# A hand-written order of attention and feed-forward work is rewritten behind its first 204 operations; weights' sums go in halves to two engines, two norms are ended on VectorE

## The chip, the cores and the metric

The kernel runs on one core of one Trainium2 chip. Its engines are PE (TensorE, matrix products; its weight loads are listed as PEld), DVE (VectorE), ACT (ScalarE), POOL (GpSimd) and SP (SyncE, which here only issues DMAs). Each engine takes its own instructions strictly in the order in which the program issued them, and waits at one whose data are not there. The metric is the device time of one execution in microseconds.

## The reference, cut to what matters

```python
# q, k, v: (8, 12, 448, 64); w_in: (768, 2048); w_out: (2048, 768)
q_n = q / (np.linalg.norm(q, axis=-1, keepdims=True) + 1e-06)
k_n = k / (np.linalg.norm(k, axis=-1, keepdims=True) + 1e-06)
scores = np.matmul(q_n, k_n.transpose(0, 1, 3, 2)) / tau          # tau = 0.1
scores = scores - np.max(scores, axis=-1, keepdims=True)
attn = np.exp(scores)
attn = attn / (np.sum(attn, axis=-1, keepdims=True) + 1e-09)
x = np.matmul(attn, v)             # its 12 heads side by side: (3584, 768)
h = x @ w_in
g = h * np.clip(h + 3.0, 0.0, 6.0) / 6.0
out = g @ w_out
```

## The kernel before, in words

**Attention.** The 8 x 12 heads are worked as 48 pairs, numbered 0 to 47, six to a batch. Queries and keys of two neighbouring pairs are loaded together as one "twin" item j, in even and odd j (`load_qk`, LQ). Values are loaded for two pairs (`load_v`, LV). For an item, the squares are taken (`square`, SQ, on the engine that the plan names: a = ACT, p = POOL, v = DVE), summed on DVE (`reduce`, RE), and turned into reciprocal norms for two items at once by four ACT activations, logarithms and exponentials (`norms`, NO, L252 to L255). The raw item is multiplied by them (`normalise`, NM), and transposed: up to item 13 by PE (`transposes`, TR, then copies out of PSUM, CQ for queries, CK and CS for keys), from item 14 on by a DMA (`crossbar`, XD, issued by SP, then CK on DVE and CS on POOL, L372). `vcast` (VC) makes the bf16 values.

For pair i there are four groups of scores, SC.i.0 to SC.i.3. Each of the first three is two matmuls of 64 rows each that run side by side; the fourth is one of 128 rows. `exps` (EX, ACT) follows each, two instructions for each of the first three groups and one for the fourth; `values` (VA, PE) multiplies by the values into the one bank PV, eight matmuls a group; `finish_values` (FI, DVE) divides and makes the bf16 output `on`. That is transposed into xT, the input of the first product, by PE and a copy (BK, CX) or by DMA (XB for one pair, XP for two).

**Feed-forward.** `unit` (U) is PE's next piece of the two products with w_in and w_out. In the plan there are 36: U1 to U30 are six matmuls of 448 columns each (L566), followed by one ACT instruction (UA, L575) and one DVE instruction (UV, L581). U31 to U36 are sixteen matmuls of 384 columns each (L613), copied out in turn by ACT (UA, L624) and by DVE (UV, L626) and stored by two DMAs from SP. UA and UV take the oldest unfinished unit. Later, in the loop, the second product is worked with sums of blocks of g and of w_out (`g_sum`, L717, and `weight_sums`, WS, L688), seven products in place of eight. `weight_sums` makes three arrays, 6, 1 and 7, and overwrites two blocks of w_out in place, y3 and y4; y3 overwrites columns that U31 to U33 read, y4 columns that U34 to U36 read. The second half of y4 is made in the loop (L861).

**PSUM.** Behind OPEN (L925), every score group (two banks, or one for the fourth), unit, TR and BK takes the next of six banks in turn: M0, M1, Y, Z, M2, M3, and again. PE can write one only when the last reader of what stood there is through.

**What sets the order.** `PLAN` (L21) is a list of 611 operations written out by hand, run one after another by `run` (L959). The program's order on each engine follows from it alone. It ends in the turn of pair 17. A loop over the pairs 18 to 47 follows, whose order is fixed in code, with the units of each pair from `TURNS` (L853) and the sums from `side`. DP.n is n dummy matmuls into an unused part of PV (L921). W issues the next part of the weights on POOL's queue. GL copies left-over columns of g.

Of the kernel before, what the change touches and what calls it, by code (L numbers as in the profile page):

```python
# [10 lines left out]
AF = mybir.ActivationFunctionType  # L11
# [3 lines left out]
EPS = 1e-6  # L15
# [46 lines left out]
def kernel(  # L62
# [10 lines left out]
    nc = tc.nc  # L73
    B, H, S, D = q.shape
# [29 lines left out]
    KC = FCN // 2  # L104
# [34 lines left out]
    def raw_buffer(j):  # L139
# [104 lines left out]
    def norms(d, *items):  # L244

        needs(("NM", 2 * d - 4), ("NM", 2 * d - 3))
        items = items or (0, 1)
        for x in items:
            needs(("RE", 2 * d + x))
        it = slice(items[0], items[-1] + 1)  # L250
        ln, nr, le, r = (t[:, it, :] for t in rs[d % 2])
        nc.scalar.activation(out=ln, in_=n2s[d % 2][:, it, :], func=AF.Ln)  # L252
        nc.scalar.activation(out=nr, in_=ln, func=AF.Exp, scale=0.5)
        nc.scalar.activation(out=le, in_=nr, func=AF.Ln, bias=EPS)
        nc.scalar.activation(out=r, in_=le, func=AF.Exp, scale=-1.0)  # L255
        for x in items:
            issued.add(("NO", d, x))

# [411 lines left out]
            return wide[n % 2], wide[2]  # L670
        return wide_late[2 * (n - LOOP) : 2 * (n - LOOP) + 2]

    def weight_sums(what, c0, n):

        w = w_out_sb[:, :, :].rearrange("p (c k) m -> p c k m", k=2)[:, c0 : c0 + n]
        b11, b12, b21, b22 = (w[:, :, k, m] for k in range(2) for m in (LEFT, RIGHT))
        for x in {"y3": "16", "y4": "17"}.get(what, ""):
            assert all((x, c) in summed for c in range(c0, c0 + n))
        o, x, y, op = {
            "1": (b11, b11, b22, ALU.add),  # L680
            "6": (b11, b11, b12, ALU.add),
            "7": (b21, b21, b22, ALU.add),
            "y3": (b12, b12, b22, ALU.subtract),
            "y4": (b21, b21, b11, ALU.subtract),
        }[what]
        if what in w_sum:
            o = w_sum[what][:, c0 : c0 + n, :]
        nc.vector.tensor_tensor(out=o, in0=x, in1=y, op=op)  # L688
# [250 lines left out]
    def whole_units(n, engines="av"):  # L939
# [153 lines left out]
```

## Time and profile before

| what | value |
|---|---|
| median of the runs shown | 405.85 us (405.72 to 407.1, 3 runs) |
| the profiled execution's own time | 405.02 us |
| its span, first to last instruction | 403.24 us |
| granted TensorE clock over the span | 1.00 |
| SC.6.0, the first matmul of the plan's ring of six banks, starts | 34.96 us |
| SC.18.0, the loop's first score matmul, starts | 114.64 us |
| last PE unit of the plan (U36) starts | 111.70 us |
| ACT, square of one item | 0.95 us, x8 |
| POOL, square, and product, of one item | 1.69 and 1.72 us, x36 and x44 |
| DVE, product of one item | 1.09 us, x2 |
| DVE, sums of weights (L688), wholes and halves | 0.95 to 3.24 us, x7 |

Durations are of one execution. A mean in the table of groups covers all instructions of one line and shape. In a timeline, each line gives start, length, engine, line, operation, what is written and read, the shape and the number of instructions merged; in brackets stands idle time before it and who ended it. An instruction's length is from its start to its end, so two that follow at once can overlap a little in it: an exponential is listed with 0.565 us, and the next starts 0.42 after it. In a list of waits stand the engine that waited, what it wanted to write, the engine that came last, and microseconds, times and the longest.

### The profile page before, as it was taken

How to read it: one execution, taken by the hardware profiler on the slowest of the kernel's cores; microseconds unless marked ns; L12 is line 12 of the kernel's file. 1: busy time of each engine (PE TensorE's matmuls, PEld its weight loads, DVE VectorE, ACT ScalarE, POOL GpSimd, SP SyncE). 2: the span in 40 equal slices, each digit the busy share in tenths (PEclk: the TensorE clock that was granted, in tenths of full speed). 3: DMA queues.
4: the chain of work that ended last, by engine and by line, in shares of the span. 5: the costliest groups of instructions: out<-in, count | busy, mean ns of one | idle time of the engine just before them, and what ended most of it. 6: DMA issues, size and time to landing. Idle time of an engine off the chain costs nothing.

```text
span 403.2 us, 9617 instructions
## 1 busy us (share of the span) xinstructions
PE 394.5 (98%) x3696; PEld 233.7 (58%) x3696; DVE 286.4 (71%) x501; ACT 266.2 (66%) x609; POOL 233.2 (58%) x228
## 2 busy tenths in 40 slices
PE   7999999999989999999999999999999999999996
PEld 5666556555655556555555556555565556555564
DVE  6898768766998676776857878687656666644663
ACT  6899998787557686776758768668648755224230
POOL 7899664562294996489386875776665500510070
PEclk9999999999999999999999999999999999999999
DMA  8999989989989559885989659986864523130133
GB/s 290 308 241 276 200 249 239 144 126 221 193 204 231 120 119 228 176 224 130 181 214 210 134 143 171 183 193 145 191 150 82 112 46 67 40 79 20 27 73 99
DMA packets 91566, 65.32 MB, mean 162 GB/s; under 512 B 56064, under 2 KB 89984, under 8 KB 91520
## 3 DMA queue, kind: packets, MB, share of 16 engines
q1 hardware_dynamic: 87408, 58.02, 62.8%
q0 software_dynamic: 3712, 6.29, 9.1%
q8 instruction: 29, 0.48, 0.5%
q10 hardware_dynamic: 400, 0.39, 0.3%
q14 instruction: 17, 0.14, 0.1%
HBM read 47.19 MB, written 11.01 MB: 144 GB/s over the span
## 4 chain that ended last, share of the span: by engine, by line
PE 94%; DVE 3%; DMA 1%; POOL 1%; ACT 0%; issue 0%; SPq 0%; DVEq 0%
PE M L566 24%; PE M L739 17%; PE PV L455 13%; PE Y L566 6%; PE M L415 6%; PE Z L566 5%; PE Y L739 4%; PE Z L739 4%; PE M L613 3%; PE M L819 2%; PE Z L415 2%; PE PV L921 2%; PE Z L819 1%; PE Y L415 1%; PE SC L415 1%; DMA big<-in_q_dram 1%
## 5 line engine op out<-in xcount | busy, mean ns | idle before, releaser
L433 ACT ACTIVATE at<-M 128x448 bf16<-128x448 f32 x200 | 99.6, 565 | 17.7 <-PE M L415 15.5
L566 PE MATMUL M<-xT,w_in_sb 128*128 128x448 bf16 x522 | 110.7, 353 | 0.0
L566 PEld LDWEIGHTS <-w_in_sb 128*128 128x128 bf16 x768 | 71.9, 98 | 62.5 <-issue 2.6
L267 POOL TENSOR_TENSOR nrm<-big,r 128x896 bf16<-128x896 f32 (+1 forms) x48 | 79.4, 1658 | 26.7 <-ACT r L255 18.5
L581 DVE SCALAR_TENSOR_TENSOR gT<-u,M 128x448 bf16<-128x448 bf16 x76 | 46.8, 618 | 35.6 <-ACT u L575 35.3
L455 PEld LDWEIGHTS <-at 128*128 128x128 bf16 (+1 forms) x1536 | 54.8, 97 | 24.1 <-issue 14.8
L224 POOL TENSOR_TENSOR big<-big 128x896 f32<-128x896 f32 (+3 forms) x39 | 63.8, 1639 | 8.0 <-DMA big<-in_k_dram 4.1
L575 ACT ACTIVATE u<-M 128x448 bf16<-128x448 f32 x87 | 48.8, 561 | 29.5 <-PE M L566 29.1
L455 PE MATMUL PV<-vx,at 128*128 128x65 bf16 (+1 forms) x1536 | 64.3, 194 | 0.2 <-DVE on L476 0.2
L236 DVE TENSOR_REDUCE n<-big 128x14 f32<-128x896 f32 (+1 forms) x50 | 51.8, 1040 | 3.9 <-ACT big L222 3.4
L372 POOL COPY km<-tT 64x128 bf16<-64x128 bf16 x34 | 12.4, 364 | 59.3 <-DMA tT<-nrm 43.4
L768 POOL TENSOR_TENSOR big<-big 128x384 f32<-128x384 f32 x11 | 12.0, 1088 | 55.1 <-ACT big L787 55.0
L739 PEld LDWEIGHTS <-gT 128*128 128x128 bf16 x288 | 27.8, 98 | 20.2 <-DVE gT L717 0.6
L739 PE MATMUL M<-w_out_sb,gT 128*128 128x384 bf16 x208 | 37.9, 326 | 0.1
L433 ACT ACTIVATE at<-Z 128x448 bf16<-128x448 f32 x49 | 27.6, 564 | 10.4 <-PE M L415 8.8
L286 POOL CAST vx<-big 128x512 bf16<-128x512 f32 x44 | 33.0, 754 | 2.4 <-DMA big<-in_v_dram 2.4
L476 DVE TENSOR_TENSOR on<-PV,rc 128x512 bf16<-128x512 f32 x48 | 33.2, 691 | 1.7
L415 PE MATMUL M<-tT,kz 64*128 64x448 bf16 (+1 forms) x175 | 31.9, 351 | 1.0 <-DVE o L626 1.0
L739 PEld LDWEIGHTS <-gs 128*128 128x128 bf16 x224 | 21.6, 98 | 14.5
L566 PE MATMUL Y<-xT,w_in_sb 128*128 128x448 bf16 x132 | 28.6, 353 | 0.0
L433 ACT ACTIVATE at<-Y 128x448 bf16<-128x448 f32 x45 | 25.6, 568 | 3.3 <-PE Z L415 3.1
L739 PE MATMUL M<-w_sum,gs 128*128 128x384 bf16 x144 | 26.3, 326 | 0.0
(131 smaller groups left out, 553.9 us busy)
## 6 DMA issues: line engine op xcount, KB each, us to landing
big<-in_v_dram SPq DMA_DIRECT2D x96, 128.0 KB, 4.7
big<-in_k_dram SPq DMA_DIRECT2D x24, 448.0 KB, 4.9
big<-in_q_dram SPq DMA_DIRECT2D x24, 448.0 KB, 4.3
out_dram<-o SPq DMA_DIRECT2D x107, 96.0 KB, 2.2
w_in_sb<-in_moe_w_in_dram POOLq DMA_DIRECT2D x4, 768.0 KB, 9.1
w_out_sb<-in_moe_w_out_dram POOLq DMA_DIRECT2D x4, 768.0 KB, 9.7
tT<-nrm SPq DMA_TRANSPOSE x34, 3.4
xT<-on SPq DMA_TRANSPOSE x25, 3.8
```

Of the source, the lines that this page charges most:

```text
L224: engines[e].tensor_tensor(out=o, in0=i, in1=i, op=ALU.mult)
L236: nc.vector.tensor_reduce(out=n2s[d % 2][:, j % 2, c], in_=sq[:, :, :, :].rearrange("p g c d -> p (g c) d")[:, c, :], axis=AX.X, op=ALU.add,)
L267: engines[e].tensor_tensor(out=nrm[:, :, g, :].rearrange("p c g d -> p g c d"), in0=raw_of[j][:, g, :, :], in1=rs[d % 2][3][:, j % 2, :] . ...
L286: (engines[e].copy if e == "a" else engines[e].tensor_copy)(out=o, in_=f)
L415: nc.tensor.matmul(o, ks, qt[rows], start=True, stop=True)
L433: nc.scalar.activation(out=o, in_=x, func=AF.Exp, scale=inv_tau)
L455: nc.tensor.matmul(pv_out(j, h), at[rows, n, q_cols(i // HP, j)], vt[rows, 3 + h if name == "M" else 5 * h + int(name[1]), :], start=(name ...
L476: nc.vector.tensor_tensor(out=on[:, :, :, :].rearrange("p j h d -> p h j d"), in0=pv4[:, :, :, 0:D], in1=rc[:, :, :].to_broadcast([128, 2, ...
L566: nc.tensor.matmul(ps[:, 0:S], w_in_sb[:, cc, fc * 128 : (fc + 1) * 128], x[:, cc, 0:S], start=(cc == 0), stop=(cc == CC - 1),)
L575: nc.scalar.activation(out=u[:, :], in_=ps[:, 0:S], func=AF.Relu, bias=0.5, scale=1.0 / 6.0)
L581: nc.vector.scalar_tensor_tensor(out=g[:, fc, c0 : c0 + S], in0=u[:, :], scalar=1.0, in1=ps[:, 0:S], op0=ALU.min, op1=ALU.mult,)
L739: nc.tensor.matmul(m, lhs[:, c, :], rhs[:, c, c0 : c0 + width], start=(base is None and c == 0), stop=(c == KC - 1), skip_group_check=True,)
```

## The change

The plan's first 204 operations, up to OPEN, stay. The 407 behind them become 411 in another order. Two dummy operations (DP.2, DP.1, three matmuls) are left out. Several copies, casts and squares go to another engine: CX.3, CX.10, CK.9, CK.13, CS.11, CS.12 from DVE to ACT; CQ.11, CK.12 from ACT to DVE; VC.8, 7, 11, 14, 16 from POOL to DVE and VC.13, 15, 17, 18, 19 from POOL to ACT; SQ.13, SQ.15 from ACT to POOL; SQ.14 from POOL to ACT and, a seventh of it, DVE; SQ.16 wholly to POOL; SQ.19, SQ.21 from POOL to ACT and SQ.22 from DVE to ACT; NM.12 from POOL to DVE, NM.11 in two halves. The norms of the twins 6 and 8 take two steps on ACT (NA) and two on DVE (ND). The sums 1, 6 and y3 are made in halves, as 7 and y4 were, and the first halves of 6 and 7 are made on POOL. The loop is not changed.

```diff
-    "BK.3.Y VA.4.1 LQ.12 CS.6.v OPEN DP.2 CX.3.v NO.5 SC.6.0 VA.4.2 VA.4.3 SC.6.1 SC.6.2 EX.6.0 NM.8.p FI.4 EX.6.1",
-    "EX.6.2 SC.6.3 TR.8 BK.4 VA.5.0 CX.4.v VA.5.1 CQ.8.v SC.7.0 VA.5.2 EX.6.3 NM.9.p CQ.9.v VC.6.p VA.5.3 SC.7.1",
-    "FI.5 EX.7.0 SC.7.2 TR.9 SC.7.3 NM.10.p CK.8.v VA.6.0 EX.7.1 EX.7.2 VC.8.p CS.8.v W BK.5 SQ.12.p.0.7 LQ.13",
-    "VA.6.1 VA.6.2 SC.8.0 EX.7.3 CS.9.v VA.6.3 CK.9.v DP.1 EX.8.0 CX.5.v SC.8.1 SC.8.2 VC.7.p FI.6 LQ.15 EX.8.1 U",
-    "UA SQ.13.a.0.7 LV.5 U TR.10 EX.8.2 UA U RE.13 U SC.8.3 UV UA CQ.10.v VA.7.0 W RE.12 UV CQ.11.a UV UA NO.6 U",
-    "EX.8.3 VA.7.1 VA.7.2 UV VC.9.p VA.7.3 NM.11.p SC.9.0 FI.7 NM.12.p UA SC.9.1 UV EX.9.0 U VA.8.0 SC.9.2 EX.9.1",
-    "VC.10.p UA SC.9.3 TR.11 UV NM.13.p CS.11.v XP.6 VA.8.1 LQ.14 EX.9.2 SQ.15.a.0.7 VA.8.2 U EX.9.3 CK.11.v",
-    "CK.10.v VA.8.3 SC.10.0 TR.12 U CS.10.v FI.8 UA UV VA.9.0 SC.10.1 LQ.17 EX.10.0 SQ.14.p.0.7 CQ.12.v CQ.13.v",
-    "SC.10.2 UA VA.9.1 LQ.19 VA.9.2 EX.10.1 LQ.16 VA.9.3 LV.6 W UV SC.10.3 EX.10.2 U SC.11.0 FI.9 EX.10.3 SC.11.1",
-    "U UA EX.11.0 LV.7 EX.11.1 UV UA SC.11.2 RE.15 BK.8 LQ.18 CX.8.v U VA.10.0 U VA.10.1 UA EX.11.2 UV UV RE.14",
-    "SC.11.3 UA BK.9 VA.10.2 VA.10.3 FI.10 EX.11.3 TR.13 NO.7 CK.13.v CS.13.v CX.9.a U UV CK.12.a VC.11.p W",
-    "VA.11.0 U SC.12.0 CS.12.v VA.11.1 VA.11.2 UA BK.10 VA.11.3 UV UA NM.15.p UV EX.12.0 CX.10.v SC.12.1 EX.12.1",
-    "SC.12.2 FI.11 U EX.12.2 BK.11 SC.12.3 UA NM.14.p SQ.16.p.0.6 U UA CX.11.v UV U SC.13.0 SQ.17.p.0.7 XD.14 UV",
-    "RE.17 EX.12.3 VC.12.p EX.13.0 SQ.16.a.6.1 U UA RE.16 VC.15.p U VA.12.0 UV XD.15 UA U UA UA UV SC.13.1",
-    "SQ.19.p.0.7 VC.13.p SC.13.2 UV EX.13.1 LQ.21 U VA.12.1 VA.12.2 UA UV RE.19 VA.12.3 EX.13.2 UV NO.8 W U",
-    "SC.13.3 NM.16.p CK.15.v CK.14.v U UA UA SQ.18.a.0.7 EX.13.3 U SC.14.0 FI.12 UA VA.13.0 VC.14.p CS.14.v UV",
-    "VA.13.1 UV EX.14.0 UV U SC.14.1 SC.14.2 VA.13.2 VA.13.3 UA EX.14.1 UV U W SC.14.3 FI.13 U VA.14.0 NM.17.p UA",
-    "EX.14.2 UA VA.14.1 EX.14.3 XD.17 U UV VA.14.2 RE.18 SC.15.0 SC.15.1 UA UV EX.15.0 U XD.16 EX.15.1 UA UV",
-    "VA.14.3 SC.15.2 U UA SC.15.3 EX.15.2 FI.14 NO.9 LV.8 VA.15.0 LV.9 UV CK.16.v UV EX.15.3 U SQ.21.p.0.7 VA.15.1",
-    "RE.21 CS.16.v LQ.20 SC.16.0 LQ.22 SC.16.1 UA VC.16.p SC.16.2 VC.17.p VA.15.2 EX.16.0 VA.15.3 XP.12 NM.18.v",
-    "CK.17.v XD.18 U EX.16.1 SQ.20.a.0.7 NM.19.p FI.15 WS.6 U UV XD.19 SC.16.3 RE.20 GL.0 WS.1 WS.7.0 EX.16.2 U VA.16.0 UA VA.16.1 LV.11",
-    "EX.16.3 SC.17.0 UV VC.19.p SC.17.1 SC.17.2 SQ.22.v.0.7 VA.16.2 LQ.23 EX.17.0 VA.16.3 EX.17.1 LV.10 U SC.17.3",
-    "XP.14 NO.10 FI.16 NM.20.p CK.18.v U CK.19.v WS.7.1 WS.y3 WS.y4.0 XB.16 EX.17.2 UV UA VA.17.0 VC.18.p EX.17.3 RE.22 CS.18.v",
+    "BK.3.Y VA.4.1 LQ.12 CS.6.v OPEN NO.5 CX.3.a SC.6.0 VA.4.2 EX.6.0 VA.4.3 FI.4 SC.6.1 EX.6.1 NM.8.p SC.6.2",
+    "EX.6.2 TR.8 SC.6.3 BK.4 VA.5.0 NM.9.p VA.5.1 VA.5.2 EX.6.3 SC.7.0 CQ.9.v VA.5.3 CQ.8.v EX.7.0 CX.4.v SC.7.1",
+    "EX.7.1 SC.7.2 TR.9 FI.5 CK.8.v SC.7.3 VC.6.p VA.6.0 CK.9.a VA.6.1 NM.11.p.1 EX.7.2 W EX.7.3 BK.5 CS.8.v",
+    "CX.5.v VA.6.2 CS.9.v VA.6.3 VC.8.v U UA UV SC.8.0 W EX.8.0 SC.8.1 U VC.7.v EX.8.1 UA NM.10.p U U SC.8.2 FI.6",
+    "UA VA.7.0 LQ.13 TR.10 UA EX.8.2 UV NM.11.p.0 SQ.12.p.0.7 UV SC.8.3 UV CQ.11.v VA.7.1 VA.7.2 CQ.10.v SC.9.0",
+    "SC.9.1 RE.12 LQ.14 SQ.13.p.0.7 EX.8.3 SC.9.2 VA.7.3 EX.9.0 U EX.9.1 FI.7 LV.5 SC.9.3 TR.11 U UA VC.11.v",
+    "CK.10.v CK.11.v CS.10.v VA.8.0 EX.9.2 UV VA.8.1 VA.8.2 EX.9.3 UA XP.6 UV SC.10.0 CS.11.a VC.9.p VA.8.3 RE.13",
+    "SC.10.1 SC.10.2 EX.10.0 EX.10.1 NA.6 U U VC.10.p UA EX.10.2 FI.8 SQ.14.v.6.1 VA.9.0 ND.6 NM.12.v SC.10.3 UA",
+    "VA.9.1 VA.9.2 NM.13.p EX.10.3 LQ.16 UV TR.12 U UV CQ.13.v VA.9.3 SC.11.0 CQ.12.v LQ.15 UA SC.11.1 U FI.9",
+    "EX.11.0 VA.10.0 VA.10.1 VA.10.2 EX.11.1 UV UA SC.11.2 EX.11.2 SQ.15.p.0.7 LV.6 VA.10.3 U SQ.14.a.0.6 LQ.17",
+    "UA UV VC.13.a BK.8 U FI.10 LQ.18 SC.11.3 UA U BK.10 LQ.19 CX.8.v EX.11.3 VA.11.0 VC.12.p UA UV RE.14 TR.13",
+    "RE.15 UV W BK.9 CX.10.a VA.11.1 CK.13.a VA.11.2 CK.12.v VA.11.3 U LV.7 CX.9.a CS.12.a UV CS.13.v FI.11 UA",
+    "SC.12.0 SC.12.1 U UV EX.12.0 BK.11 UA SQ.17.p.0.7 CX.11.v W NO.7 SQ.16.p.0.7 U UV EX.12.1 U RE.16 UA VA.12.0",
+    "SC.12.2 UA SQ.18.a.0.7 UV U NM.15.p EX.12.2 UA U RE.17 UV SC.12.3 VA.12.1 UV VA.12.2 NA.8 UA EX.12.3 UV",
+    "NM.14.p U SC.13.0 UA SQ.19.a.0.7 SC.13.1 XD.14 U UV EX.13.0 U GL.0 VC.15.a UA VA.12.3 ND.8 EX.13.1 UV UA",
+    "FI.12 U UV SC.13.2 NM.16.p UA UV U CK.14.v RE.18 UA U EX.13.2 SC.13.3 UV XD.15 VA.13.0 VA.13.1 CK.15.v W U",
+    "EX.13.3 UA UA SC.14.0 U CS.14.v EX.14.0 UV LQ.22 UA UV LQ.20 W VA.13.2 SQ.20.a.0.7 VC.14.v VA.13.3 SC.14.1",
+    "XD.16 NM.17.p UV SC.14.2 FI.13 U EX.14.1 U VA.14.0 SC.14.3 VA.14.1 EX.14.2 XD.17 UA UA RE.20 EX.14.3 SC.15.0",
+    "U VA.14.2 LV.8 EX.15.0 VA.14.3 WS.1.v.0 UA UV UV SC.15.1 FI.14 LQ.21 SC.15.2 U EX.15.1 WS.6.p.0 LV.9 UV",
+    "WS.6.v.1 SC.15.3 U RE.19 CK.16.v VA.15.0 VA.15.1 UV XP.12 WS.1.v.1 EX.15.2 UA WS.7.v.1 NO.9 SC.16.0 SC.16.1",
+    "CK.17.v EX.15.3 SC.16.2 EX.16.0 VA.15.2 SQ.21.a.0.7 NM.18.v WS.7.p.0 VA.15.3 CS.16.v FI.15 EX.16.1 EX.16.2",
+    "XD.18 U VC.19.a SC.16.3 U NM.19.p VC.16.v XD.19 UA EX.16.3 VA.16.0 WS.y3.v.0 LV.10 VA.16.1 RE.21 SC.17.0",
+    "VC.18.a LQ.23 SC.17.1 UV EX.17.0 EX.17.1 NO.10 SC.17.2 EX.17.2 VA.16.2 VC.17.a VA.16.3 CK.18.v U XP.14",
+    "WS.y3.v.1 SC.17.3 U FI.16 SQ.22.a.0.7 UA WS.y4.v.0 XB.16 UV NM.20.p RE.22 CK.19.v EX.17.3 VA.17.0 CS.18.v",
+    "LV.11",
...
+    def powers(d, *items):
+
+        needs(("NM", 2 * d - 4), ("NM", 2 * d - 3))
+        items = items or (0, 1)
+        for x in items:
+            needs(("RE", 2 * d + x))
+        it = slice(items[0], items[-1] + 1)
+        ln, nr = (t[:, it, :] for t in rs[d % 2][:2])
+        nc.scalar.activation(out=ln, in_=n2s[d % 2][:, it, :], func=AF.Ln)
+        nc.scalar.activation(out=nr, in_=ln, func=AF.Exp, scale=0.5)
...
+    def reciprocals(d, *items):
...
+        nr, le, r = (t[:, it, :] for t in rs[d % 2][1:])
+        nc.vector.tensor_scalar_add(out=le, in0=nr, scalar1=EPS)
+        nc.vector.reciprocal(out=r, in_=le)
...
-    def weight_sums(what, c0, n):
+    def weight_sums(what, c0, n, e="v"):
...
-        nc.vector.tensor_tensor(out=o, in0=x, in1=y, op=op)
+        engines[e].tensor_tensor(out=o, in0=x, in1=y, op=op)
```

In `WS.6.p.0` the letter names the engine and the last number the half (four of eight pairs of row blocks, 1536 columns); `NM.11.p.1` is the second half of an item.

More of the change, by code (lines that the diff above doesn't have):

```diff
@@ L255, in norms @@
         nc.scalar.activation(out=r, in_=le, func=AF.Exp, scale=-1.0)
+        for x in items:
+            issued.add(("NO", d, x))
+    def powers(d, *items):
+        needs(("NM", 2 * d - 4), ("NM", 2 * d - 3))
+        items = items or (0, 1)
+        for x in items:
+            needs(("RE", 2 * d + x))
[3 more added lines that the diff above has]
+        nc.scalar.activation(out=nr, in_=ln, func=AF.Exp, scale=0.5)
+        for x in items:
+            issued.add(("NA", d, x))
+    def reciprocals(d, *items):
+        items = items or (0, 1)
+        for x in items:
+            needs(("NA", d, x))
+        it = slice(items[0], items[-1] + 1)
+        nr, le, r = (t[:, it, :] for t in rs[d % 2][1:])
+        nc.vector.tensor_scalar_add(out=le, in0=nr, scalar1=EPS)
+        nc.vector.reciprocal(out=r, in_=le)
         for x in items:
@@ L946 @@
     OPS = {
-        "LQ": load_qk, "LV": load_v, "W": next_weights, "SQ": square, "RE": reduce, "NO": norms,
+        "LQ": load_qk, "LV": load_v, "W": next_weights, "SQ": square, "RE": reduce, "NO": norms, "NA": powers, "ND": reciprocals,
         "NM": normalise, "VC": vcast, "TR": transposes, "XD": crossbar, "XB": back_crossbar, "XP": back_two, "CQ": copy_q, "CK": copy_k, "CS": copy_k3, "SC": scores,
         "EX": exps, "VA": values, "FI": finish_values, "BK": back, "CX": copy_x, "U": unit, "UA": lambda: finish_units("a"), "UV": lambda: finish_units("v"),
-        "GL": g_left, "WS": lambda x, *h: weight_sums(str(x), *((h[0] * KC // 2, KC // 2) if h else (0, KC))), "UU": whole_units, "D": busy, "DP": busy_pv, "OPEN": open_ring,
+        "GL": g_left, "WS": lambda x, e, *h: weight_sums(str(x), *((h[0] * KC // 2, KC // 2) if h else (0, KC)), e), "UU": whole_units, "D": busy, "DP": busy_pv, "OPEN": open_ring,
     }
@@ L955, in do @@
         key = (op,) + tuple(a for a in args if isinstance(a, int))
-        if op not in ("RE", "NM", "LQ"):
+        if op not in ("RE", "NM", "LQ", "NA", "ND"):
             issued.add(key[:3] if op == "SC" else key)
```

## The prediction

> **What bounds the kernel now.** I read the page's busy line first, then the stages, then who waited for whom on PE, then the timeline around the longest wait.
>
> ```profile
> PE 394.5 (98%) x3696; PEld 233.7 (58%) x3696; DVE 286.4 (71%) x501; ACT 266.2 (66%) x609; POOL 233.2 (58%) x228
> ```
>
> PE is busy nearly always. "Busy" alone could hide waits, as matmuls overlap, so I took the recorded starts of neighbouring matmuls. In a unit of six 448-column products they lie 0.189 us apart, in one of 384 columns 0.1625, in the value products 0.029, again and again with no spread to speak of. So between 34.66 us, where the changed orders part, and the end PE runs without gaps except where a wait is listed. The list for PE from 34 to 122 us has one line:
>
> ```profile
> PE M L415 <- DVE o L626: 1.0, 1, 1.0
> ```
>
> Its place:
>
> ```profile
> 111.34 4.52 DVE L688 TENSOR_TENSOR w_out_sb<-w_out_sb 128x3072 bf16<-128x3072 bf16 x2
> 111.70 2.76 PE L613 MATMUL M<-w_out_sb,gT 128*128 128x384 bf16 x16
> ...
> 115.03 0.35 PE L415 MATMUL M<-tT,kz 64*128 64x448 bf16 x1
> ...
> 115.79 0.54 DVE L626 COPY o<-M 128x384 f32<-128x384 f32 x1
> ...
> 116.39 0.35 PE L415 MATMUL M<-tT,kz 64*128 64x448 bf16 x1 [1.01 <-DVE o L626]
> ```
>
> PE's 36th unit (U36) ends near 114.47. Its bank is copied out by DVE (L626) only behind y3 whole and y4's first half, 4.52 us of sums, and the last score matmul of SC.18.2 needs that bank: it starts at 116.39 instead of 115.03 + 0.19, **1.17 us late**. That is all that can be won by waiting less, up to the later waits of 0.17 (near 120.84) and 0.30 us (near 225). Before 56 us another engine is nearly as full:
>
> ```profile
> 30.00:40.00 10.00, 9.96 (x162) 6.76 (x161) 8.14 (x24) 9.75 (x21) 9.99 (x11) 1.00 1.10 276
> ...
> 100.00:110.00 10.00, 10.00 (x90) 6.20 (x89) 9.60 (x12) 4.84 (x11) 3.33 (x2) 1.00 1.00 208
> ```
>
> After the length come PE, PEld, DVE, ACT, POOL: ACT 9.75 of 10 us there; DVE 9.60 at 100 us, with POOL idle.
>
> **PE's own work.** Both orders hold the same scores, values, transposes and units. The new one leaves out DP.2 and DP.1, three dummy matmuls at 0.106 us: -0.32. Score pairs that stand alone cost a change of shape on both sides: values to scores starts 0.34 us apart against 0.245 for values to values, and scores to values 0.285 against 0.19, 0.19 us per run of scores. Counted in the two orders there are 22 runs before, 21 after: -0.19. Together **-0.50 us**. The floor is no lower than that.
>
> **The first waits.** Without DP.2, SC.6.0 starts at 34.75 (VA.4.1 at 34.41 plus 0.34), and SC.6.1 is due at 34.75 + 0.29 + 2 x 0.245 + 0.10 = 35.63. It writes bank Y, which CX.3 reads. CX.3 was DVE's (35.20 to 35.59) and goes to ACT behind NO.5, whose last instruction starts at 35.12: from about 35.3 with 0.51 us (the one ACT cast to xT) it ends at 35.81, and SC.6.1 starts near 35.86, 0.23 late. Then TR.8, due 35.86 + 0.20 + 0.29 = 36.35, needs NM.8, the second of
>
> ```profile
> 33.12 3.33 POOL L267 TENSOR_TENSOR nrm<-big,r 128x896 bf16<-128x896 f32 x2
> ```
>
> which ends at 36.45 whatever the order: 0.13 to 0.17 late. BK.4 needs the bank that EX.6.1 frees, pushed back by 0.43 on ACT: 0.05. Sum **+0.41 us**: the dummies covered these waits, and leaving them out wins nothing. CK.9 on ACT adds 0.38 before EX.7.2; NO.6 (four steps of 0.26) comes later as two, SQ.13 (0.84) goes to POOL. Following the exponentials at 0.425 each, banks come back 0.0 to 0.3 us ahead of PE until U1, and U5 waits about 0.07. U1 itself comes 0.3 us before CX.5 is done, but only its sixth matmul, 0.95 us on, reads that part of xT: nothing. With ACT this full, a pace 2% off over 10 us adds 0.2, so I keep +0.2 to +0.9 for this part, and take +0.48.
>
> **Norms ended on VectorE.** NA takes two ACT steps (0.52 in place of 1.04); ND is an addition and a reciprocal of 28 columns on DVE, not seen here; nearest is the reciprocal of 8 columns (206 ns), upper end the 614 ns of a 448-column reduce. I take 0.2 each, 0.44 with gaps, twice. NM.12 follows at once on DVE (1.0) and ends about 0.1 us before TR.12 needs it; at the upper end (0.8 more) TR.12 would wait 0.7. [...] NA.8 and ND.8 have 3 us of slack before NM.16.
>
> **Copies moved among DVE, ACT, POOL.** VC on DVE is 0.68 (L284), on ACT about 0.5 (from the 0.94 for 896 columns), each beside PE work of over a microsecond before its values are due. SQ.21 and SQ.22 on ACT stand where ACT was 4.84 to 6.18 of 10 busy. SP issues the same DMAs; XD.14 holds SP until NM.14 (near 75.4), and LQ.22 and LQ.20 behind it land (4.5 us median) some 5 us before SQ.20 asks. LV.11 moves to the end of the plan, its four issues (2.6 us) ahead of XB.17, which has 1.5 us to spare. I cost all this at nothing; if one cover fails it is 0.2 to 0.5 us.
>
> **The sums in halves.** WS on DVE took 1.7 to 2.65 us whole, 0.95 for a half. The difference is POOL:
>
> ```profile
> 99.56 1.68 POOL L267 TENSOR_TENSOR nrm<-big,r 128x896 bf16<-128x896 f32 x1
> 99.60 0.69 DVE L476 TENSOR_TENSOR on<-PV,rc 128x512 bf16<-128x512 f32 x1
> 100.21 2.65 DVE L688 TENSOR_TENSOR w_sum<-w_out_sb 128x3072 bf16<-128x3072 bf16 x1
> 101.19 2.14 POOL L286 CAST vx<-big 128x512 bf16<-128x512 f32 x1
> ```
>
> The sum ends 1.62 us after POOL's product ends (101.24), and POOL's cast (0.61 elsewhere) ends 0.47 after the sum (102.86). The two engines take turns; DVE's product with an input in PSUM (99.60) is not held. [...]
>
> So a POOL half of 1536 columns costs DVE whatever it overlaps. POOL has no such row. From below: products of 448 and 896 columns take 0.94 and 1.68, 0.2 + 1.65 ns a column, 2.7 us. From above: four times the 1.0 of 384 columns with two separate inputs (L768), 4.0. I take 3.4 (0.2 + 4 x 0.8), the row with separate inputs being nearest in kind. [...]
>
> When? Both p halves wait for nothing but POOL's queue: from ND.8 (79.8), NM.16, W, CS.14, W, NM.17 are 1.63 + 0.75 + 0.6 + 0.75 + 1.63 = 5.4, so they run from 85.2 to 85.2 + 2 x 3.4 = 92.0. DVE reaches WS.1.v.0 behind FI.13 and RE.20 at about 91.0, is held 1.0, and the two UV behind it free the bank of SC.15.1 that much later; they had 0.83 to spare. **+0.2 us** (0 at 2.7, +1.4 at 4.0). CS.16 behind them is wanted 9 us later.
>
> **The end.** y3 now lies before U36 in halves (y3.0 at 105, y3.1 at 108). What holds the bank of U36 is y4.0. It overwrites w_out's first chunks, and its compiled wait is on U36's eighth matmul, not its last. In the old trace this can't be seen, as y3 ended at 114.50. The eighth ends 1.5 us after U36's start, y4.0 takes 0.87 alone, so it is over before U36 ends (+2.77); then the copy, 0.54, and 0.06: the bank is free 3.40 after U36's start, PE wants it at 3.33. Left of 1.17: 0.1. **-1.07 us.**
>
> **Sum.** -0.50 + 0.48 + 0.20 - 1.07 = -0.89. The profiled execution (405.02, span 403.24) would come to 404.1; the median of the runs shown lies 0.83 above it, so 405.0 on that scale.
>
> **Rivals.**
> 1. No new wait appears: -0.50 - 1.17, and with the later 0.17 -1.84: 404.0. Against it: NM.8's end at 36.45 is fixed. 0.12.
> 2. The change doesn't do what it says: y4.0 waits for all of U36. Then 0.87 + 0.54 follow 114.47's counterpart, the stall is 0.9 to 1.0 us, and the sum near 0: 405.9. For it: y4.0's start at 114.50 fits U36's end too. 0.12.
> 3. Slower: POOL's halves hold DVE. Place: WS.1.v.0 before the two UV; price 2p - 6.6 us for a half of p us. From p = 3.9 it eats the gain; at 4.5 (L768's longest is 1.5 for 384, so not excluded) it is 2.4 and the time 407.1; over 408 from p = 5.0. For it: the turns in the rows above. Against: 0.94 for 448. 0.14.
> 4. My sum holds: 0.62.
>
> About 0.5% (2.03 us) is what a measurement can tell here. Faster by more, under 403.8, needs rival 1 and a later wait too: 0.06. Slower by more, over 407.9: part of rival 3 and several failed covers at once: 0.11. Within: 0.83. Range 403.8 to 407.5, from rival 1 to rival 3, with the bounds of the first waits and of p.
>
> **What would show it.** Right: PE's list from 34 to 122 us with no wait over 0.3; SC.6.1 behind ACT's cast; TR.8 at about 36.5; SC.18.2's last matmul near 115.1; POOL's L688 at 2.7 to 4.0. Wrong: y4.0 starting at U36's end; DVE's L688 near 91 over 2.5 us with PE waiting at SC.15.1; ACT idle on DVE or DMA at NA, SQ.20 or VC.

## The result, and the profile after

The changed kernel takes **408.15 us** (median of 20 executions, 406.1 to 411.37), the kernel before 405.66 (20, 405.19 to 407.46): ratio **1.0054**, 95% interval 1.0038 to 1.0070, slower. The forecast was 405.0, within 403.8 to 407.5. The profiled execution of after took 408.19 us, span 406.2, mean granted clock 0.994.

The profile page's busy line says little here: PE is busy 1.3 us longer with three matmuls fewer.

```profile
PE 395.8 (97%) x3693; PEld 234.4 (58%) x3693; DVE 286.4 (71%) x506; ACT 269.7 (66%) x617; POOL 229.4 (56%) x219
```

PE's list of waits, from 30 to 142 us, has one line again, but another one. (In the changed file the lines of these operations stand 27 lower: U is L593, scores L442, sums of weights L715; in experiments that lose a line of the plan, 26.)

```profile
PE M L593 <- DMA xT<-on: 2.4, 1, 2.4
```

The old wait is gone, by the mechanism that the forecast gave. The timeline around U36 (start, length, engine, line, operation):

```profile
111.78 2.76 PE L640 MATMUL M<-w_out_sb,gT 128*128 128x384 bf16 x16
...
113.35 0.96 DVE L715 TENSOR_TENSOR w_out_sb<-w_out_sb 128x1536 bf16<-128x1536 bf16 x1 [2.87 <-POOL km L399]
...
114.63 0.56 DVE L653 COPY o<-M 128x384 f32<-128x384 f32 x1 [0.33 <-PE M L640]
...
115.11 0.48 PE L442 MATMUL M<-tT,kz 64*128 64x448 bf16 x2
```

y4.0 starts 1.2 us before U36 ends, just behind U36's eighth matmul (the bracket names a copy on POOL that ended just then; in e12 y4.0 starts 0.1 us behind the eighth matmul again, and 0.3 before that copy ends). The copy follows U36 and not the sum, and SC.18.2's last two matmuls are merged into one line: nothing stands between them. The second of them starts at 115.25; before it was 116.39.

The new wait is 10 us later, at the first unit that reads the part of xT which XB.17 transposes. The timeline of PE there:

```profile
124.70 1.11 PE L593 MATMUL M<-xT,w_in_sb 128*128 128x448 bf16 x5
128.23 0.50 PE L593 MATMUL M<-xT,w_in_sb 128*128 128x448 bf16 x1 [2.42 <-DMA xT<-on]
128.53 2.44 PE L593 MATMUL Y<-xT,w_in_sb 128*128 128x448 bf16 x6
```

Five matmuls run, the sixth waits: its start is 2.77 us behind the fifth's, where 0.189 is usual. And then six matmuls take 2.44 us. In the kernel before the same six took 1.30:

```profile
126.91 1.30 PE L566 MATMUL Y<-xT,w_in_sb 128*128 128x448 bf16 x6
```

The stages of the changed kernel show why (length, busy time of PE, PEld, DVE, ACT, POOL, granted clock, then the DMA engines' share and GB/s; the clock is 1.00 ahead of these):

```profile
125.00:130.00 5.00, 2.58 (x10) 0.98 (x8) 1.42 (x4) 2.13 (x8) 0.71 (x3) 0.83 1.08 223
130.00:135.00 5.00, 5.00 (x45) 2.62 (x44) 2.72 (x5) 2.23 (x6) 5.00 (x5) 0.83 0.95 280
135.00:140.00 5.00, 5.00 (x42) 2.85 (x39) 3.55 (x6) 3.57 (x9) 4.76 (x5) 1.00 0.57 131
```

Behind the wait, eight matmuls start 0.373 us apart instead of 0.189, and one on either side of them 0.29: TensorE ran at half its clock for 3.41 us (granted clock 0.50 from 128.30 to 131.71), and ten intervals took 3.57 us instead of 1.89, **1.68 us** more.

**How the kernels are compared below.** PE's first wait, for the first loads near 10 us, was 0.1 to 2.3 us in the profiles of this study, in code that no kernel here changes. So beside medians I give the *stretch*: from one and the same matmul ahead of the changed orders (33.42 us before, 33.60 after) to the last matmul. Before 365.63, after 368.38: **+2.75**. At the unit above the changed kernel was 1.25 ahead of the one before (124.70 and 125.77, less 0.18 of a later start). Then come +2.58 of waiting and +1.68 of half clock, together +3.01; the remaining -0.26 is won behind it, where the old wait near 225 us (0.30) does not come back. A stretch has scatter of its own: two profiles of one kernel (e3 and e12) differ by 0.65, and kernels that are the same up to 110 us (e1, e2, e6, e7, e13) lose up to there 0 to 1.1 us more than the changed kernel's profile. So a smaller difference than that is read from the waits named beside it. One execution each of e10, e13 and e14 was in a slower state (411.4, 413.1 and 409.97 us): it counts in the medians, not in the ratios.

**Why XB.17 is late** shows in SP's issues. First of before (98.35 is its first output store, the last line XB.17), then of after:

```profile
98.35 1.20 SPq L601 DMA_DIRECT2D out_dram<-o  x2
...
121.45 1.21 SPq L507 DMA_TRANSPOSE xT<-on  x1
```

```profile
96.12 1.72 SPq L209 DMA_DIRECT2D big<-in_v_dram  x2
100.93 1.18 SPq L628 DMA_DIRECT2D out_dram<-o  x2
...
120.89 2.66 SPq L209 DMA_DIRECT2D big<-in_v_dram  x4
123.59 0.59 SPq L197 DMA_DIRECT2D big<-in_k_dram  x1
124.29 1.22 SPq L534 DMA_TRANSPOSE xT<-on  x1
```

XB.17's landing takes the same time (4.0 us before, 3.9 after); the issue is 2.84 us later. From its first store on SP is nearly always issuing, 23.1 us to XB.17 before and 23.4 after, the same transfers in both. But the run starts 2.6 us later. Up to 97.85 SP issues loads; then it stands until 100.93, because in the new order U32's store (its copy on DVE ends at 100.9) is ahead of U31's (copied by ACT at 98.0):

```profile
97.49 0.48 ACT L651 COPY o<-Z 128x384 f32<-128x384 f32 x1 [1.05 <-PE Z L640]
...
100.35 0.56 DVE L653 COPY o<-M 128x384 f32<-128x384 f32 x1 [2.46 <-PE M L640]
```

Theories. **T1**: LV.11's own new place, with its four issues (2.66 us) among the last things ahead of XB.17, makes it late. **T2**: SP is full from its first store on; what counts is when that run starts and how much lies in it, and LV.11 was in it before too. **C1**: the half clock follows from PE's standing still. **C2**: it has another reason.

### The profile page after: what moved, and what is told of

Same layout as the page of the kernel before. It is cut to its first block, busy times and chain, and to the rows that moved or that the text cites. A ratio compares the mean times of both kernels' runs of the same rounds, so it can differ in the third digit from the quotient of the medians.

```text
span 406.2 us, 9628 instructions
## 1 busy us (share of the span) xinstructions
PE 395.8 (97%) x3693; PEld 234.4 (58%) x3693; DVE 286.4 (71%) x506; ACT 269.7 (66%) x617; POOL 229.4 (56%) x219
## 4 chain that ended last, share of the span: by engine, by line
PE 91%; DVE 3%; DMA 2%; ACT 2%; POOL 0%; issue 0%; SPq 0%; ACTq 0%
PE M L593 24%; PE M L766 16%; PE PV L482 12%; PE Y L593 6%; PE M L442 5%; PE Z L593 5%; PE Y L766 4%; PE Z L766 3%; PE M L846 2%; PE M L640 2%; PE Z L442 1%; ACT at L460 1%; PE Z L640 1%; PE Y L442 1%; DMA big<-in_k_dram 1%; PE PV L948 1%
## 5 line engine op out<-in xcount | busy, mean ns | idle before, releaser
L593 PE MATMUL M<-xT,w_in_sb 128*128 128x448 bf16 x522 | 110.6, 353 | 2.4 <-DMA xT<-on 2.4
L593 PEld LDWEIGHTS <-w_in_sb 128*128 128x128 bf16 x768 | 72.4, 98 | 66.9 <-issue 7.7
L226 POOL TENSOR_TENSOR big<-big 128x896 f32<-128x896 f32 (+2 forms) x38 | 62.4, 1645 | 11.5 <-DMA big<-in_q_dram 5.4
L442 PE MATMUL M<-tT,kz 64*128 64x448 bf16 (+1 forms) x171 | 31.5, 351 | 0.0
L593 PE MATMUL Y<-xT,w_in_sb 128*128 128x448 bf16 x138 | 31.0, 362 | 0.0
L460 ACT ACTIVATE at<-Y 128x448 bf16<-128x448 f32 x47 | 26.6, 565 | 3.4 <-PE Z L442 3.3
L313 POOL CAST vx<-big 128x512 bf16<-128x512 f32 x34 | 24.1, 712 | 1.9 <-DMA big<-in_v_dram 1.4
```

The lines of the kernel that those rows point to most:

```text
L226: engines[e].tensor_tensor(out=o, in0=i, in1=i, op=ALU.mult)
L313: (engines[e].copy if e == "a" else engines[e].tensor_copy)(out=o, in_=f)
L442: nc.tensor.matmul(o, ks, qt[rows], start=True, stop=True)
L460: nc.scalar.activation(out=o, in_=x, func=AF.Exp, scale=inv_tau)
L593: nc.tensor.matmul(ps[:, 0:S], w_in_sb[:, cc, fc * 128 : (fc + 1) * 128], x[:, cc, 0:S], start=(cc == 0), stop=(cc == CC - 1),)
```

## The experiments

Stretches are of one profile each; "half clock" counts executions whose mean granted clock was 0.996 or lower, wherever in the execution it fell (in the profiles of e4, e5 and e10 behind the first loads). XB.17's issue is given less the lag of that profile's PE behind the changed kernel's at the same matmul between 116 and 119 us (in e5, behind the kernel before's at 115). In e10 and e14 this lag takes in a wait of PE's just ahead of it; counted ahead of that wait, XB.17 stands at 121.5 and 119.4. The kernel before was run again beside each group of experiments (medians 405.3 to 405.7; 3 of 34, 2 of 23 twice, 1 of 29 and 0 of 22 of its executions show 0.996 or lower).

| kernel | median us (n) | ratio, 95% interval | stretch less before's | XB.17 issued | PE's wait for it | half clock |
|---|---|---|---|---|---|---|
| after | 408.15 (20) | 1.0054, 1.0038 to 1.0070 | +2.75 | 124.3 | 2.4 | 11 of 20 |
| LV.11 back (e1) | 408.46 (8) | 1.0049, 1.0019 to 1.0079 | +2.02 | 123.7 | 2.1 | 2 of 8 |
| LV.11 behind XB.17 (e2) | 406.49 (10) | 1.0029, 1.0010 to 1.0048 | +2.31 | 121.3 | 0 (another: 1.9) | 1 of 10 |
| LV.10, LQ.23 early (e3) | 405.53 (10) | 0.9986, 0.9967 to 1.0005 | -1.02 | 121.6 | 0.2 | 0 of 10 |
| the same again (e12) | 406.19 (12) | 0.9997, 0.9970 to 1.0025 | -0.37 | 122.0 | 0.8 | 3 of 12 |
| U31's store first (e4) | 405.56 (10) | 1.0008, 0.9980 to 1.0036 | +0.44 | 123.0 | 1.2 | 3 of 10 |
| e3 and e4 together (e8) | 405.66 (12) | 1.0001, 0.9978 to 1.0023 | +0.04 | 122.0 | 0.6 | 1 of 12 |
| before, LV.11 last (e5) | 406.65 (10) | 1.0025, 1.0005 to 1.0046 | +0.09 | 122.5, before 121.45 | 0 | 1 of 10 |
| XD.20 ahead of XB.17 (e6) | 409.86 (9) | 1.0093, 1.0063 to 1.0123 | +5.87 | 125.4 | 4.3 | 8 of 9 |
| wait filled (e7) | 407.45 (10) | 1.0043, 1.0018 to 1.0067 | +1.80 | 123.8 | 0.9 | 0 of 10 |
| e3 and e1 together (e9) | 405.17 (12) | 1.0000, 0.9984 to 1.0016 | -0.53 | 122.1 | 0.6 | 1 of 12 |
| e9, halves on DVE (e10) | 405.89 (12) | 0.9996, 0.9978 to 1.0015 | +0.09 | 121.0 | 0 (others: 0.8) | 2 of 12 |
| e3, LQ.24 behind (e11) | 406.63 (12) | 1.0018, 0.9989 to 1.0046 | +2.06 | 121.4 | 0 (another: 1.9) | 3 of 12 |
| **LV.11 behind XD.21 (e13)** | **404.36 (12)** | **0.9969, 0.9948 to 0.9991** | **-1.12** | 121.3 | 0 | 1 of 12 |
| e13 and e3 together (e14) | 404.92 (12) | 0.9984, 0.9958 to 1.0010 | +0.63 | 117.4 | 0 (another: 1.6) | 2 of 12 |

**e1, LV.11 back at its earlier place.**

```diff
-... VA.16.3 CK.18.v U XP.14
+... VA.16.3 CK.18.v U LV.11 XP.14
...
-    "LV.11",
```

> The changed kernel with one operation back where it stood before: LV.11 stands ahead of XP.14 again, not at the end of the plan. T1 (LV.11's own late place puts its four issues, 2.66 us, ahead of XB.17): the 2.42-us wait of TensorE for XB.17's chunk is gone, and the time is about 404. T2 (SP is full from the first output store on, and LV.11 lies ahead of XB.17 in either place): XB.17 is issued at 124.3 within 0.5 us as in the changed kernel, the wait stays at 2.4 within 0.4, and the time is that of the changed kernel, 408.

XB.17 was 0.6 us sooner, the wait 2.1 us instead of 2.4, and the time that of the changed kernel. T1 falls: LV.11's place explains a fifth of the 2.84 us.

**e2, LV.11 behind XB.17.** The loop calls `do("LV", 11)` right behind `do("XB", 17)`; the plan's last line goes.

> The changed kernel with LV.11 taken from the plan and issued by the loop right behind XB.17. Both T1 and T2 expect XB.17 to be issued 2.66 us sooner, at about 121.6, and the wait of 2.42 us gone, unless the load of V is then late itself. What it tells apart is what the wait is worth. C1 (the clock of 0.83 from 125 to 135 us follows from TensorE's standing still in that wait): the clock stays at 1.0 and the time falls by the wait and the lost clock together, 2.4 + 1.7 = 4.1, to about 404.0. C2 (the clock falls there for another reason, as the denser stage ahead of it): the time falls by the wait alone, to about 405.7, and the records show 0.83 again.

XB.17 came 3.0 us sooner and its wait went, but 1.9 us of another wait appeared at 137 us: PE's product waits for an addition on DVE (L822). So this run prices nothing cleanly, and it says that a second thing is due behind XB.17. It is named under e11.

**e3 and e12, LV.10 and LQ.23 in SP's idle stretch.**

```diff
-... VA.15.0 VA.15.1 UV XP.12
+... VA.15.0 VA.15.1 LV.10 LQ.23 UV XP.12
```

They are taken out further on, between WS.y3.v.0 and SC.17.1.

> The changed kernel with LV.10 and LQ.23 (2.66 + 0.7 us of issues) moved ahead of U32's output store, into the stretch from 97.9 to 100.9 us in which SP stands idle waiting for that store's copy. LV.11 keeps its late place. T2 (SP's unbroken run of issues from the first store to XB.17 is what makes XB.17 late): some 3 us of issues leave the run, XB.17 is issued at about 121.3, the wait is below 0.3, and the time is about 404 to 405. T1 (LV.11's place): nothing changes, the wait stays at 2.4 and the time at 408.

T2 holds: LV.11 stands late as in the change, yet XB.17 is issued 2.7 us sooner and the wait is 0.2 us.

> The kernel of the third experiment once more (LV.10 and LQ.23 ahead of U32's store), for an interval narrower than 0.9967 to 1.0005 and a second profile: a stretch of 364.6 within 0.3 and a wait of 0.2 to 0.8 if the first profile was typical, a ratio of 0.997 to 0.999.

The second profile had 0.8 us of the wait and a stretch of 0.37 below before's (365.26, outside the 364.6 within 0.3), and the ratio missed its range too; the medians (405.53, 406.19) lie on both sides of before's. So this edit takes the loss away and no more that can be measured.

**e4, U31's store ahead of U32's.**

```diff
-... UV XP.12 WS.1.v.1 EX.15.2 UA WS.7.v.1
+... EX.15.2 UA UV XP.12 WS.1.v.1 WS.7.v.1
```

> The changed kernel with U31's copy and store (ScalarE, ready at 97.7) put ahead of U32's copy and store (VectorE, ready at 100.9) in the order of the program. T2: SP has a store to issue at 97.9 instead of 100.9, so 1.2 us of stores go out in the idle stretch and XB.17 is issued at about 123.1; the wait falls from 2.4 to about 1.2, and the time to some 405.5 to 407. T1: the wait stays at 2.4 and the time at 408.

The wait fell to 1.2 us and XB.17 by 1.3, as T2 put it in numbers: the order of two stores, with not one instruction added, is worth 1.2 us of wait at a unit some 25 us later.

**e5, the kernel before with LV.11 last.**

> The kernel before with only LV.11 taken to the end of the plan, as the change does. T1 (LV.11's late place alone made XB.17 late): 1.2 us of wait appear at the first unit that reads XB.17's chunk, about 407. T2 (LV.11 was ahead of XB.17 already, so its place within the run changes nothing): XB.17 is issued at 121.4 within 0.5 us, no wait, and the time is that of the kernel before, 405.7 within 0.7.

No wait appeared, and the stretch is before's within 0.1. XB.17 came 1.0 us later, not within 0.5 as T2 had it: without LV.11 to issue, SP stood 1.2 us for U35's and U36's data. It used up the slack of before and no more. The median is above before's all the same; in this profile the wait for the first loads was 2.0 us, in that of before 0.74, but that this explains the median is not shown.

**e6 and e7, what the wait does to the clock.** In e6 the loop issues XD.20 ahead of XB.17; in e7 twenty unread matmuls (`do("DP", 20)`) stand ahead of the waiting unit.

> The changed kernel with one more transfer, XD.20 (some 1.3 us of issue), ahead of XB.17. T2: XB.17 is issued 1.3 us later, at about 125.6, and TensorE's wait grows from 2.4 to 3.7 us. C1 (a wait of some 2.5 us or more brings the matmuls behind it to half the clock for about 3.5 us, a shorter one doesn't): the ten or more matmuls behind the wait take 0.37 us instead of 0.19, in the profile and by the mean clock in nearly all runs, and the time is some 409 to 410. C2 (the clock has nothing to do with the wait): half the clock no oftener than in the changed kernel, and 408 to 409.5.

> The changed kernel with twenty matmuls that nobody reads (2.1 us) ahead of the unit that waits for XB.17's chunk; the wait's end isn't moved, TensorE is only busy in most of it. C1 (the standing still brings the half clock): the stretch behind it runs at full clock, 1.8 us are won over a profile of the changed kernel that shows the half clock, and the median is 406.3 to 407.3. C2 (something else lowers the clock there): ten matmuls at 0.37 us again in the profile or in half of the runs, and 408.

PE's timeline with the longer wait, and then with the filled one:

```profile
132.28 0.53 PE L593 MATMUL M<-xT,w_in_sb 128*128 128x448 bf16 x1 [4.33 <-DMA xT<-on]
132.61 2.44 PE L593 MATMUL Y<-xT,w_in_sb 128*128 128x448 bf16 x6
```

```profile
126.38 2.28 PE L948 MATMUL PV<-xT 128*128 128x248 bf16 x20
...
130.55 0.35 PE L593 MATMUL M<-xT,w_in_sb 128*128 128x448 bf16 x1 [0.95 <-DMA xT<-on]
130.74 1.30 PE L593 MATMUL Y<-xT,w_in_sb 128*128 128x448 bf16 x6
```

With 4.33 us of standing still the next six matmuls take 2.44 us, with 0.95 us they take 1.30. By executions: none of ten show the lower mean clock where PE was kept busy, 8 of 9 with the long wait, 11 of 20 with the wait of 2.4. C2 falls: filling the wait with useless work made the kernel 0.95 us shorter in its stretch. It is not the whole 1.7, as XB.17 landed 4.8 us after its issue here and not 3.9, which moved the wait's end 0.4 us later. C1 holds in that standing still brings the half clock; its bound of "some 2.5 us" is put more closely in the last section. The wait in e6 was 4.3, not the expected 3.7, and e7's median is 0.15 above its range, as 0.95 of the wait stayed where 0.3 was expected.

**e8 and e9, two edits together.** e8 joins e3 and e4, e9 joins e3 and e1.

> The changed kernel with both edits that took issues out of SP's unbroken run: LV.10 and LQ.23 ahead of U32's store, and U31's copy and store ahead of U32's. T2: XB.17 is issued at 121 within 0.7 us (counted from the same start), the wait for its chunk is gone to the last 0.1 (it was 0.23 with the first edit alone and 1.37 with the second alone), and the records show full clock behind it. Counted from a matmul behind the start-up loads to the last one it should be 1.0 to 1.3 us shorter than the kernel before (the first edit alone: 1.03), so a median of 404.5 to 405.2 beside 405.7. If instead another wait takes the place of this one, it is no shorter than the first edit alone.

> The changed kernel with LV.10 and LQ.23 ahead of U32's store and, besides, LV.11 ahead of XP.14, in a second stretch (113.1 to 114.3 us of the run with the first edit alone) in which SP waited for a copy. T2 with both places counted: XB.17 is issued at 120 to 121.5 (121.9 with the first edit alone), nothing of the wait is left, and from the matmul that ends the first 33 us to the last matmul it is 364.3 to 364.7 us (before 365.63, the first edit alone 364.61): a median of 404.6 to 405.4. If LV.11 there waits for its buffer or delays XP.14 in its turn, it shows as a new wait of TensorE at a unit of batch 1, and the stretch is 365 or more.

Both missed: XB.17 stood at 122.0 and 122.1, no sooner than with e3 alone. The issues became longer. LV.9 and LV.10 back to back took 7.46 us in e9 for eight issues, 0.93 each, where LV.10 in its later place took 2.66 for four, 0.67 each; LV.11 took 3.35 us in e8. So what fills SP's idle time is partly given back. Full DMA engines are not all of the reason: at 94 to 100 us their mean share was 1.13 in the changed kernel and 1.13 from 94 to 102 us in e9, but 0.57 from 115 to 120 us in e8, where LV.11 was longer too. The cause was not tried and stays open.

**e10, e9 with the two GpSimd halves on VectorE** (`WS.6.p.0` and `WS.7.p.0` become `.v.0`).

> The same kernel, and the two halves of the weights' sums that GpSimd makes (3.08 us each, beside which VectorE's own halves took up to 1.36 instead of 0.95) are made by VectorE. My prediction gave GpSimd's halves +0.20 us by the hold on VectorE. If that hold costs TensorE nothing, as the trace of the changed kernel reads, the stretch is the other kernel's plus whatever two more VectorE sums of 0.95 us push back: 0 to +0.6. If the hold costs 0.2, the stretch is 0.2 shorter.

The stretch is 0.62 longer than e9's, just over the upper end of what two more sums push back, and 0.8 us of waits for a DVE copy (L652) appear at SC.17 and SC.18. So nothing speaks for a hold on VectorE that costs TensorE time. That GpSimd's halves are worth having is likely by these waits, but not shown: 0.62 is no more than two profiles of one kernel differ by, and the medians can't tell (0.9996 and 1.0000).

**e11, e3 with LQ.24 behind XB.17.**

> The changed kernel with LV.10 and LQ.23 ahead of U32's store, and LQ.24 (0.6 us of issue, the last thing ahead of XB.17) behind XB.17. XB.17 stood at 121.9 to 122.05 in three kernels whose runs of issues began at 98, 102 and 102.5 us, so what stands far ahead of it seems to be made up by longer issues; what stands right ahead of it isn't. If so, XB.17 is issued 0.6 us sooner, at 121.3, the wait is gone (0.23 to 0.8 in those three), and the stretch from the matmul that ends the first 33 us to the last matmul is 364.2 to 364.7 us (before 365.63): a median 0.5 to 1.2 below the kernel before. If XB.17 waits for its data and not for SP, it stays at 121.9 and the wait stays.

XB.17 came 0.3 to 0.6 us sooner than in e3 and e12 and its wait was gone, but the stretch is 2.06 longer than before's. About half of that is waits near 55 us in this profile, ahead of anything that was moved. What is left is the wait of e2, and this time I followed it back (timeline of all engines):

```profile
131.11 0.64 POOL L399 COPY km<-tT 64x128 bf16<-64x128 bf16 x2 [9.44 <-DMA tT<-nrm]
...
139.21 0.99 POOL L796 TENSOR_TENSOR big<-big,o 128x384 f32<-128x384 f32 x1
140.24 0.56 DVE L823 TENSOR_TENSOR big<-Y,big 128x384 f32<-128x384 f32 x1 [2.64 <-POOL big L796]
140.85 1.46 PE L766 MATMUL Y<-w_sum,gs 128*128 128x384 bf16 x8 [1.93 <-DVE big L823]
```

Read upwards: PE waits for DVE, DVE for POOL's addition, and POOL, which has no pause from 131.1 on, had stood 9.44 us for tT, the transfer XD.20. That is SP's next transposing issue behind XB.17. Less the lag of this profile's PE, 2.9 us, the km copies start at 128.2; by the same count they start at 127.2 in e12, and at 126.4 in the kernel before. So **SP has two things due at the end of its run**, and an issue moved from in front of XB.17 to behind it is still in front of XD.20. In e11 that is only part of the cause: XD.20 was issued at 123.3, no later than in e12, but took 4.8 us to land where it took 3.8 there (why is open), and PE, no longer held by XB.17, came 0.8 us sooner. In e2, with LV.11 between the two, XD.20 was issued at 125.3 and landed in 3.5: there SP alone made it late.

**e13 and e14, LV.11 behind both.** What was open: whether XD.20 and XB.17 explain the whole loss, and whether the predicted gain was there at all.

```diff
         if even:
             prepare(("XD", i + 3))
+            if i == FIRST:
+                do("LV", 11)
```

The plan's last line goes. Against e2, LV.11 has only moved from behind XB.17 to behind XD.20 and XD.21.

> The changed kernel with LV.11's four issues (2.66 us) behind XB.17, XD.20 and XD.21, all of which TensorE waits for directly or by way of GpSimd; nothing else moved. If SP's run of issues ahead of these three is what costs the time (T2, with two things due at its end: XB.17, and XD.20, whose landing starts GpSimd's work for the products at 136 us), both are 2.4 to 2.7 us sooner, XB.17 at 121.7 and XD.20 at 123.0 as in the kernel before (121.45 and 122.76), the wait of 2.42 is below 0.7, the wait at 136 below 0.6, the half clock is rare, and the stretch from the matmul that ends the first 33 us to the last one is 364.7 to 365.6 (before 365.63, changed 368.38). If the fifth and eleventh experiments' second wait (2.1 us at 138) had another reason than XD.20's lateness, it is there again and the stretch is above 367.

SP's issues of e13, and PE's unit that waited:

```profile
121.54 1.20 SPq L533 DMA_TRANSPOSE xT<-on  x1
122.83 2.65 SPq L349 DMA_TRANSPOSE tT<-nrm  x2
```

```profile
124.74 1.30 PE L592 MATMUL M<-xT,w_in_sb 128*128 128x448 bf16 x6
```

XB.17 and the two items behind it are issued at the times of before (121.45 and 122.76), the six matmuls run without a wait, PE's list of waits from 30 to 142 us is empty, and the kernel is **faster than before: 404.36 against 405.31, ratio 0.9969 (0.9948 to 0.9991)**. The stretch is 1.12 us below before's, a little more than the range I gave. The second wait of e2, 1.9 us at 137 us, is gone as well. One load, moved, turns the slower order into the faster one.

> The same, and LV.10 and LQ.23 ahead of U32's store besides. T2: XB.17 at 118.5 to 119.5 and XD.20 at 120 to 121, no wait at either place; what is left of the predicted gain is then all there: a stretch of 364.3 to 364.7, that is 0.9 to 1.3 below the kernel before, and a median 0.6 to 1.3 below its median. If it is not shorter than 365.3, the first waits and the end that I predicted at -0.89 together were read wrongly, not only SP.

Counted ahead of the new wait, XB.17 went to 119.4 as expected. But in the profile the gain is gone: a wait of 1.6 us stands at SC.18.2, the place of the old one.

```profile
112.17 2.48 DVE L714 TENSOR_TENSOR w_out_sb<-w_out_sb 128x1536 bf16<-128x1536 bf16 x1
...
115.41 2.31 DVE L714 TENSOR_TENSOR w_out_sb<-w_out_sb 128x1536 bf16<-128x1536 bf16 x1
...
117.64 0.55 DVE L652 COPY o<-M 128x384 f32<-128x384 f32 x1
```

The two halves, 0.95 us each elsewhere, took 2.48 and 2.31, beside POOL's product (112.14, 1.69 us) and copies (113.78, 1.37 us) and its next square and product. In the same kernel DVE had stood 2.8 us for a transposed item just ahead of them. I expected no wait in either place. It is not the work of this edit: PE's wait begins at 116.6 us, and e14 differs from e3 only in LV.11, which SP issues from 118.0 us on in e3. In e3 and e12, too, DVE stood 1.9 and 2.2 us for that transposed item (0.36 in the changed kernel), and PE did not wait. So the loads in SP's idle stretch bring that transfer late, and in this profile the lateness reached PE. The profiled execution, 407.16 us, is not typical: six of the twelve took 403.66 to 404.63.

## Why the prediction was wrong, point by point

- **PE's own work and the first waits**: right. CX.3 on ACT, SC.6.1 behind it, NM.8 and TR.8 behind that:

```profile
33.30 3.32 POOL L294 TENSOR_TENSOR nrm<-big,r 128x896 bf16<-128x896 f32 x2
...
35.43 0.51 ACT L359 COPY xT<-Y 128x448 bf16<-128x448 bf16 x1
...
35.99 0.35 PE L442 MATMUL Y<-tT,kz 64*128 64x448 bf16 x1
...
36.48 0.56 PE L339 MATMUL M<-ident,nrm 128*128 128x128 bf16 x7
```

  Less 0.18 of a later start these are 35.81 (said 35.86) and 36.30 (said 36.35). No start gap over 0.31 follows between 39 and 119 us. At U36's start the changed kernel's PE was 0.10 ahead of the one before and e13's 0.35 behind, where +0.18 was forecast: right in so far as the scatter allows.
- **Norms ended on VectorE**: right, no wait from them.
- **The sums in halves**: the hold on DVE was there, its size too high. A POOL half took 3.08 us (I took 3.4), the pair ended at 91.73, and DVE's half, 0.95 us with POOL idle, took 1.36, held by 0.41:

```profile
85.60 6.13 POOL L715 TENSOR_TENSOR w_sum<-w_out_sb 128x1536 bf16<-128x1536 bf16 x2
...
91.19 1.36 DVE L715 TENSOR_TENSOR w_sum<-w_out_sb 128x1536 bf16<-128x1536 bf16 x1
```

  PE waited for none of it: 0 instead of +0.20. (One reading was short: whole sums took 1.75 to 3.24 us in the profile of before, as y3's 3.24 shows, not 1.7 to 2.65. Nothing rests on it.) Rival 3 needed 3.9. In e14, where other work came to lie beside the sums, DVE's halves of 2.48 and 2.31 us end at 114.65 and 117.72, each 0.82 us behind an instruction of POOL (112.14, 1.69 us, and 115.22, 1.68 us), as the half above ends 0.82 behind 91.73: in these rows the two engines take turns.
- **The end**: right. Of the wait of 1.17 nothing is left, where 0.1 was expected; y4.0 does not wait for U36 (rival 2 falls). With all that is ahead of it, SC.18.2's last matmul stands 1.32 us earlier than before, less the later start, and 0.87 in e13, where 0.89 was forecast. That e13 comes so near is partly luck, as its +0.35 and the end's -1.22 both miss their terms (+0.18, -1.07) and cancel.
- **Copies moved: the step that failed.** It said of LV.11's four issues that XB.17 "has 1.5 us to spare. I cost all this at nothing; if one cover fails it is 0.2 to 0.5 us." Two things were wrong. I took "SP issues the same DMAs" as a reason for no cost, and never laid SP's issues out in time: which store heads the run, when its data are ready (+1.2 us of wait, e4), what else lies between it and XB.17 (e3, e13). And the slack was read from the trace of before, though the same sum brought PE 0.89 us sooner to that unit, which leaves 0.6. By those numbers alone, 2.6 of issues against 0.6 of slack, the forecast would have been a wait of 2.0 us; 2.4 came. It would have had the right size for a partly wrong reason, since LV.11 lay ahead of XB.17 before too. None of the rivals had a late transfer in it.
- **No price for the clock.** Nothing in the forecast allowed a wait to cost more than its length. Where the half clock followed, in the profile of after, it cost 1.68 us on top of 2.42.
- **The sum**: -0.89 was forecast for the steps that I did price. e13, in which the unpriced one is gone, has -1.12, and -0.87 of it up to SC.18.2. The gain was there, given back 10 us after it was won.

## What to carry to other kernels

When an order is rewritten, lay out the queue that only issues DMAs as one lays out TensorE: the head of each run, whose data it waits for, and what is due at its end. A transfer's slack has to be reckoned against where the faster engine will be, and an issue moved out of one deadline's way must go behind the next one on that queue too. A wait on TensorE can cost more than its length by the clock behind it (after: 2.42 us, and 1.68 behind them), so a filled wait can be cheaper than an empty one (e7's stretch is 0.95 us shorter than after's).

## What the runs showed of the hardware that was not expected

- **The clock behind a pause.** In the profiles' clock records each stretch at half clock ahead of the last matmul lasts 3.41 us, and it starts a whole number of 3.413 us behind the profile's first record: 2 in e4, e5 and e10 (behind the wait for the first loads), 36 in after (first record at 5.42 us, half clock from 128.30), 37 in e6. So in these profiles the clock changed in steps of that length, and the first record begins somewhere between 5.2 and 8.0 us of the span. Cut all 16 profiles into these steps, from the first record to the last matmul, and sum PE's idle time in each: steps with 2.17 us or more (e4 2.17, e10 2.18, after 2.42, e6 3.41) are followed by one at half clock, steps with 1.78 us or less (e11 1.78, e1 1.68, e7 1.65 and all others) never; of the two between, e5's 1.93 is and e2's 1.94 is not. What tells them apart is how much of a pause falls into one step: after's 2.42 lies whole in one, e1's 2.14 is cut into 1.68 and 0.46 and runs free. An estimate from these figures, with a bound of 2.05 us: a pause of 2.42 reaches it in one step in (3.41 + 2.42 - 2 x 2.05) / 3.41, about half of all positions, and 11 of 20 executions of the changed kernel show the loss; one of 4.33 reaches it always, and 8 of 9 show it. So some 2 us of standing still within one step were enough here.
- **Issues of one kind differ in length.** A load of LV's four takes 0.67 us in some places (LV.11 in after) and 0.84 to 0.98 in others (0.84 for LV.11 in e8, 0.98 at 120.26 us in e11), which took back part of what e8 and e9 moved forward; why is open.
- **GpSimd's half**: 3.08 and 3.09 us for a sum of two bf16 inputs of 1536 columns in the profile of after.
